# Loading tokens in runs of 4 or 5, and token-major attention tiles with DMA transposes from batch 3 on

## The chip, the cores and the metric

One core of one Trainium2 chip. The time is the device time of one launch in microseconds (us), here always in the fast state; a kernel's time is the median of its runs. Where two kernels are compared, the ratio is the mean time of one kernel's fast runs over the mean of the other's fast runs of the same rounds on the same chip, with a 95% interval. It is therefore not quite the ratio of the medians that are quoted beside it.

## The reference, cut to what matters

```
# q, k, v: 8 batches x 8 heads x 576 tokens x 64
kv  = einsum('bhsd,bhse->bhde', k, v)
out = einsum('bhsd,bhde->bhse', q, kv)
out = out / sqrt(mean(out*out, axis=-1) + 1e-6) * g_norm     # per token and head
x   = out as 4608 tokens x 512
h   = x @ w_in                                               # 512 -> 2048
g   = max(h, 0) + alpha * min(h, 0)
y   = g @ w_out                                              # 2048 -> 512
```

576 tokens are four and a half times 128, and the kernels work through the 4608 tokens in nine windows of 512. Batches and windows therefore do not line up: a window takes its tokens from one or two batches.

## The kernel before

All matrix products are in fp16. A head pair j is 128 of the 512 features. Attention for the next window is cut into small steps, which are strewn between the MLP units of the window at hand. A step is a transpose of q on TensorE (`t`), the product of k and v (`kv`), the output product (`ot`), or the sum of squares with the normalisation (`ssq`):

```
    def step_ot(w, j, pool=None):          # features on partitions
        ...
            nc.tensor.matmul(
                out=ot_ps[:, n0 - w * W : n1 - w * W], lhsT=kvs[b, j][:],
                rhs=qts[b, j][:, n0 - b * S : n1 - b * S], start=True, stop=True,
            )
        ...
        nc.scalar.activation(out=sq[:], in_=ot_ps[:], func=AF.Square)

    def ssq_mm(w, j):                      # sum of squares over partitions: a matmul with a mask
        nc.tensor.matmul(out=ssq_ps[:], lhsT=mask16[:], rhs=sq[:], start=True, stop=True)
        ... # Ln, Exp on ScalarE
```

One unit of the MLP is four matmuls for 128 features of h, a Relu on ScalarE (`m_sb`), the PReLU on VectorE (`gt`), and four matmuls of y for the window before. The window loop pops the steps behind the units:

```
            want = n * (g - first_g + 1) // (NF - 2 - first_g)
            while steps and n - len(steps) < want:
                steps.pop(0)()
```

The start brings in batch 0 in halves of four heads and works on each half as it comes (`regroup` copies a loaded half into the order that the matmuls need; `keep_warm(n)` issues n idle matmuls, whose result nobody reads):

```
    regroup(0, "q", 0, H // 2)
    step_t(0, 0, H_POOL)
    regroup(0, "k", 0, H // 2)
    step_t(0, 1, H_POOL)
    keep_warm(3)
    step_kv(0, 0)
    step_kv(0, 1, H_POOL)
    step_ot(0, 0)
    step_ot(0, 1)
    regroup(0, "q", H // 2, H)
    ... # transposes of the second half
    ssq_mm(0, 0)
    ssq_mm(0, 1)
    norm(0, 0)
    step_kv(0, 2)
    step_kv(0, 3, H_POOL)
    norm(0, 1)
```

## Time and profile before

| | before |
|---|---|
| time | 320.44 us, median of 3 runs (319.75 to 321.03) |
| profiled run | 319.12 us, span 317.4 us, mean granted TensorE clock 0.993 |
| start of window 2 | 79.35 us |
| start of window 2 to the last run of y matmuls | 218.57 us |

The last two rows cut the run in two: a start, in which engines wait for data and for each other, and a steady stretch, in which TensorE is full. The start in a few lines of the timeline of PE (start us, busy us, engine, line, operation, output<-inputs, shape; in brackets the idle time before it and who ended it):

```profile
9.75 1.25 PE L234 MATMUL qt_ps<-ident,qsb 128*128 128x128 f16 x10 [0.60 <-DVE qsb L146]
...
12.33 0.51 PE L249 MATMUL kv_ps<-vst,ksb 128*128 128x128 f16 x4
...
18.10 0.38 PE L323 MATMUL h_ps<-xt,w_in_sb 128*128 128x512 f16 x1
```

The first q work starts at 9.75 us, the first kv product at 12.33, the MLP at 18.10. The groups of PE instructions that the change cuts (line, engine, operation, shape, count | busy us, mean ns | idle us before, by releaser):

```profile
L234 PE MATMUL qt_ps<-ident,qsb 128*128 128x128 f16 x160 | 14.4, 225 | 1.9 <-DVE qsb L146 1.2 <-DVE kv_sb L257 0.8
L287 PE MATMUL ssq_ps<-sq_sb,mask 128*128 128x512 f16 x36 | 13.6, 378 | 6.7 <-ACT sq_sb L277 5.6 <-ACT rstd L289 1.1
```

The mean ns of one matmul (225, 378) is the length of its record, and records of neighbours overlap; what one costs in a row of them is read from starts, 56 and 216 ns.

### The profile page before, as it was taken

Reading aid. Unit: us, or ns where it says so; the run is one execution under the profiler, and the core shown is the slowest. Engines: PE = TensorE matmul, PEld = TensorE weight load, DVE = VectorE, ACT = ScalarE, POOL = GpSimd, SP = SyncE. Lnnn points to the kernel's source line nnn. Section 1 sums busy time; section 2 is a strip of 40 time slices with the busy share of each in tenths; the row PEclk is TensorE's granted clock in tenths of the full one; section 3 lists DMA queues with packets and bytes.
Section 4 is the critical chain, followed back from the end, with each engine's and each line's share of the span. In section 5 each row is a group of like instructions: output and inputs, shape, how many; then the busy total and the mean of one; then the engine's idle time right before and its main releaser. Section 6 shows DMA issues by size and latency. Waiting matters only on the chain.

```text
span 317.4 us, 4195 instructions
## 1 busy us (share of the span) xinstructions
PE 293.4 (92%) x1588; PEld 142.0 (45%) x1588; DVE 157.2 (50%) x267; ACT 173.4 (55%) x292; POOL 66.6 (21%) x74
## 2 busy tenths in 40 slices
PE   5668998898999999999999999999999999999994
PEld 1323453454455455545554455444544444444441
DVE  4547833666655554545464546454554445443300
ACT  2366546468466636674567456655665667444211
POOL 8434312737340541055005200000000000000000
PEclk9799999999999999999999999999999999999999
DMA  7999999998973859077715811000011111001132
GB/s 110 179 206 195 200 197 143 174 149 89 169 101 51 115 92 118 34 104 113 108 35 86 120 35 33 33 36 33 33 35 33 33 33 36 33 34 37 52 80 66
DMA packets 47621, 28.27 MB, mean 89 GB/s; under 512 B 14304, under 2 KB 42992, under 8 KB 47600
## 3 DMA queue, kind: packets, MB, share of 16 engines
q0 software_dynamic: 40320, 18.16, 45.7%
q1 hardware_dynamic: 7280, 9.84, 11.2%
q8 instruction: 12, 0.20, 0.3%
q14 instruction: 9, 0.07, 0.1%
HBM read 36.71 MB, written 9.44 MB: 145 GB/s over the span
## 4 chain that ended last, share of the span: by engine, by line
PE 85%; ACT 6%; DVE 4%; DMA 2%; issue 1%; SPq 1%; ACTq 0%
PE h_ps L323 37%; PE y_ps L345 36%; PE qt_ps L234 3%; PE kv_ps L249 3%; PE ssq_ps L287 3%; PE ot_ps L271 2%; DMA alpha_row<-in_moe_alpha_dram 2%; ACT rstd L289 2%; ACT sq_sb L277 1%; ACT rstd L292 1%; DVE gt L332 1%; DVE xt L298 1%; ACT m_sb L330 1%; SPq L100 1%; PE yb L345 1%
## 5 line engine op out<-in xcount | busy, mean ns | idle before, releaser
L332 DVE SCALAR_TENSOR_TENSOR gt<-m_sb,beta_sb,h_ps 128x512 f16<-128x512 f32 x144 | 106.8, 745 | 87.2 <-ACT m_sb L330 86.4
L323 PE MATMUL h_ps<-xt,w_in_sb 128*128 128x512 f16 x576 | 146.2, 379 | 2.9 <-DVE xt L298 1.7
L345 PE MATMUL y_ps<-w_out_sb,gt 128*128 128x512 f16 x528 | 134.8, 379 | 0.1
L330 ACT ACTIVATE m_sb<-h_ps 128x512 f32<-128x512 f32 x144 | 85.3, 594 | 80.4 <-PE h_ps L323 80.3
L345 PEld LDWEIGHTS <-gt 128*128 128x128 f16 x576 | 56.1, 98 | 67.1 <-issue 1.7
L323 PEld LDWEIGHTS <-w_in_sb 128*128 128x128 f16 x576 | 54.2, 98 | 64.2 <-issue 10.4
L298 DVE SCALAR_TENSOR_TENSOR xt<-ot_ps,g2col,rstd 128x512 f16<-128x512 f32 x36 | 27.0, 751 | 43.3 <-ACT rstd L292 43.2
L289 ACT ACTIVATE rstd<-ssq_ps,eps_t 128x512 f32<-128x512 f32 x36 | 24.7, 687 | 18.0 <-PE ssq_ps L287 17.9
L277 ACT ACTIVATE sq_sb<-ot_ps 128x512 f16<-128x512 f32 x36 | 21.3, 596 | 16.2 <-PE ot_ps L271 15.6
L352 ACT COPY y_sb<-y_ps 128x512 f32<-128x512 f32 x33 | 19.3, 586 | 18.4 <-PE y_ps L345 18.4
L292 ACT ACTIVATE rstd<-rstd 128x512 f32<-128x512 f32 x36 | 22.7, 629 | 1.1
L287 PE MATMUL ssq_ps<-sq_sb,mask 128*128 128x512 f16 x36 | 13.6, 378 | 6.7 <-ACT sq_sb L277 5.6
L129 POOL DMA_DIRECT2D vst<-in_v_dram x9 | 7.7, 860 | 50.4 <-PE kv_ps L249 48.6
L146 POOL COPY qsb<-qst 128x2048 f16<-128x2048 f16 x6 | 11.4, 1897 | 32.5 <-DMA qst<-in_q_dram 32.5
L249 PEld LDWEIGHTS <-ksb 128*128 128x128 f16 x160 | 11.6, 99 | 11.2 <-issue 4.2
L234 PE MATMUL qt_ps<-ident,qsb 128*128 128x128 f16 x160 | 14.4, 225 | 1.9 <-DVE qsb L146 1.2
L234 PEld LDWEIGHTS <-qsb 128*128 128x128 f16 x160 | 11.6, 101 | 9.4 <-DVE qsb L146 2.4
L243 DVE COPY qt_sb<-qt_ps 128x576 f16<-128x576 f16 x32 | 14.4, 451 | 2.5 <-PE qt_ps L234 2.5
L271 PE MATMUL ot_ps<-qt_sb,kv_sb 128*128 128x512 f16 (+7 forms) x64 | 13.5, 286 | 0.8 <-DVE kv_sb L257 0.7
L249 PE MATMUL kv_ps<-vst,ksb 128*128 128x128 f16 x128 | 12.3, 220 | 1.8 <-DVE qt_sb L243 1.8
L146 POOL COPY ksb<-kst 128x2048 f16<-128x2048 f16 x6 | 11.4, 1903 | 11.9 <-DMA kst<-in_k_dram 11.9
L257 DVE TENSOR_TENSOR kv_sb<-kv_ps,mask 128x128 f16<-128x128 f32 x32 | 9.0, 285 | 3.8 <-PE kv_ps L249 3.8
(43 smaller groups left out, 92.6 us busy)
## 6 DMA issues: line engine op xcount, KB each, us to landing
out_dram<-y_sb SPq DMA_DIRECT2D x40, 128.0 KB, 2.4
out_dram<-y_sb SPq DMA_DIRECT2D x16, 256.0 KB, 2.3
kst<-in_k_dram POOLq DMA_DIRECT2D x7, 512.0 KB, 6.9
qst<-in_q_dram POOLq DMA_DIRECT2D x7, 512.0 KB, 10.1
vst<-in_v_dram POOLq DMA_DIRECT2D x7, 512.0 KB, 8.4
w_in_sb<-in_moe_w_in_dram POOLq DMA_DIRECT2D x4, 512.0 KB, 14.7
w_out_sb<-in_moe_w_out_dram POOLq DMA_DIRECT2D x4, 512.0 KB, 16.1
qst<-in_q_dram POOLq DMA_DIRECT2D x2, 256.0 KB, 7.5
```

Source lines behind the costliest of these rows:

```text
L146: (eng or nc.vector).tensor_copy(out=dst, in_=src)
L234: nc.tensor.matmul(out=qt_ps[:, t * P : (t + 1) * P], lhsT=qs(t), rhs=ident16[:], is_transpose=True, start=(t == 0), stop=(t == NT - 1),)
L249: nc.tensor.matmul(out=kv_ps[:], lhsT=ks(t), rhs=vs(t), start=(t == 0), stop=(t == NT - 1),)
L277: nc.scalar.activation(out=sq[:], in_=ot_ps[:], func=AF.Square)
L287: nc.tensor.matmul(out=ssq_ps[:], lhsT=mask16[:], rhs=sq[:], start=True, stop=True)
L289: nc.scalar.activation(out=rstd[:], in_=ssq_ps[:], func=AF.Ln, bias=eps_t[:], scale=inv_d,)
L292: nc.scalar.activation(out=rstd[:], in_=rstd[:], func=AF.Exp, bias=0.0, scale=-0.5)
L298: nc.vector.scalar_tensor_tensor(out=xts[w, j][:], in0=ot_ps[:], scalar=g2col[:], in1=rstd[:], op0=ALU.mult, op1=ALU.mult,)
L323: nc.tensor.matmul(out=h_ps[:], lhsT=w_in_blk(c, g), rhs=xts[w, c][:], start=(c == 0), stop=(c == NC - 1),)
L330: nc.scalar.activation(out=m_sb[:], in_=h_ps[:], func=AF.Relu, scale=-1.0)
L332: nc.vector.scalar_tensor_tensor(out=gt[:], in0=m_sb[:], scalar=beta_sb[:, g : g + 1], in1=h_ps[:], op0=ALU.mult, op1=ALU.add,)
L345: nc.tensor.matmul(out=y[:], lhsT=gts[w, g][:, a * P : (a + 1) * P], rhs=w_out_blk(g), start=(g == 0), stop=(g == NF - 1),)
```

## The change

Its intent: the loads become two per tensor, in which each partition takes a run of 5 tokens (the first 320 tokens) or 4 (the other 256), in place of runs of 4 and single tokens. From batch 3 on, q is transposed by a DMA instead of TensorE, the output product is made with tokens on partitions (a tile is 128 tokens x 512 features), the sum of squares becomes a reduction on VectorE, GpSimd spreads the factor `rg`, VectorE multiplies, and a second DMA transposes the tile into the layout that the MLP needs (`xm`). The loads of a batch, their regrouping and the transpose of q are placed in different units. Load buffers go from three sets to two. The start is rewritten: q of batch 0 comes uncast over SyncE's queue, and is cast on VectorE.

```
+    def load(b, nm, h0=0, h1=H, dst=None, eng=None):
+        ...
+            out=st[0:REM].rearrange("p h t d -> p h (t d)"),
+            in_=src[:, 0:LONG, :].rearrange("h (p t) d -> p h (t d)", t=NT),
+        ...
+            out=st[REM:P, :, 0:TPP, :].rearrange("p h t d -> p h (t d)"),
+            in_=src[:, LONG:S, :].rearrange("h (p t) d -> p h (t d)", t=TPP),
...
+    def transpose_q(b):
+        nc.sync.dma_start_transpose(out=qtms[b][:], in_=bufs[b % NBUF]["q"][:]...)
+
+    def tile_a(b, t):                       # four 128-column matmuls, tokens on partitions
+        ot_ps = ps_o.tile([P, H, D], FP32, name="otm_ps", tag=f"o{n_tile[0] % 3}")
+        ... # Square on ScalarE
+    def tile_b(b, t): ...                   # tensor_reduce on VectorE
+    def tile_c(b, t): ...                   # Ln, Exp on ScalarE, rg on GpSimd
+    def tile_d(b, t):
+        nc.vector.tensor_mul(out=x[0:n], in0=ot_ps[0:n], in1=rg[0:n])
+        ... # nc.sync.dma_start_transpose into xm
...
+        for i in range(len(todo) + 3):      # unit i of the window
+            m = []
+            for k, fn in ((3, tile_d), (0, tile_a), (1, tile_b), (2, tile_c)):
+                if 0 <= i - k < len(todo):
+                    m.append(lambda fn=fn, x=todo[i - k]: fn(*x))
+            d = i >= 3
+            steps.append((m[:d], m[d:]))    # (between h and y, behind y)
+        if w < B:
+            for j in range(NPAIR):
+                steps[j // 2][j % 2].append(lambda j=j: step_kv(w, j))
...
+    regroup(0, "q", 0, HH, src=q32[0])      # the start
+    step_t(0, 0, H_POOL)
+    step_t(0, 1, H_POOL)
+    regroup(0, "q", HH, H, src=q32[1])
+    step_t(0, 2, H_POOL)
+    step_t(0, 3, H_POOL)
+    regroup(0, "k", 0, HH)
+    keep_warm(3)
+    step_kv(0, 0)
+    ...
+    step_kv(0, 2)
+    step_kv(0, 3, H_POOL)
+    norm(0, 0)
+    norm(0, 1)
```

All four `kv_ps` of a window use the one PSUM buffer `(ps_s, "s")`; the tiles turn over three, `o0` to `o2`.

## The prediction

> **What bounds the kernel now.** The page's first two parts say which engine and when; the columns of the first are busy us, share of the span, instructions.
>
> ```profile
> PE 293.4 (92%) x1588; PEld 142.0 (45%) x1588; DVE 157.2 (50%) x267; ACT 173.4 (55%) x292; POOL 66.6 (21%) x74
> ...
> PE   5668998898999999999999999999999999999994
> ...
> PEclk9799999999999999999999999999999999999999
> ```
>
> PE is full from about slice 11 (80 us) on and has gaps only in the first ten slices of 7.9 us; the clock is granted everywhere but in one early slice. No other engine is near full. The chain that ended last agrees: 85% of it is PE.
>
> ```profile
> PE 85%; ACT 6%; DVE 4%; DMA 2%; issue 1%; SPq 1%; ACTq 0%
> PE h_ps L323 37%; PE y_ps L345 36%; PE qt_ps L234 3%; PE kv_ps L249 3%; PE ssq_ps L287 3%; PE ot_ps L271 2%; DMA alpha_row<-in_moe_alpha_dram 2%; ACT rstd L289 2%; ACT sq_sb L277 1%; ACT rstd L292 1%; DVE gt L332 1%; DVE xt L298 1%; ACT m_sb L330 1%; SPq L100 1%; PE yb L345 1%
> ```
>
> 73% is the MLP itself (h and y), which the change leaves alone. qt, ssq and ot, 8% together, are what it touches. The waits of PE from 79.6 us (start of window 2; a window is 512 tokens, 16 units of 4 h and 4 y matmuls) to 298 us have one entry (total us, times, longest):
>
> ```profile
> PE ssq_ps L287 <- ACT sq_sb L277: 3.4, 5, 0.7
> ```
>
> So for 218 us every PE instruction taken away shortens the run, and every new PE wait lengthens it. I read the prices from one unit of the timeline (start us, us):
>
> ```profile
> 148.49 1.03 PE L323 MATMUL h_ps<-xt,w_in_sb 128*128 128x512 f16 x4
> ...
> 149.35 1.03 PE L345 MATMUL y_ps<-w_out_sb,gt 128*128 128x512 f16 x4
> 149.55 0.60 ACT L330 ACTIVATE m_sb<-h_ps 128x512 f32<-128x512 f32 x1 [1.41 <-PE h_ps L323]
> ...
> 150.18 0.75 DVE L332 SCALAR_TENSOR_TENSOR gt<-m_sb,beta_sb,h_ps 128x512 f16<-128x512 f32 x1 [1.05 <-ACT m_sb L330]
> 150.22 0.44 PE L234 MATMUL qt_ps<-ident,qsb 128*128 128x128 f16 x5
> ...
> 150.50 1.03 PE L323 MATMUL h_ps<-xt,w_in_sb 128*128 128x512 f16 x4
> ```
>
> Starts, not durations, give the cost: four 512-column matmuls take 149.35 - 148.49 = 0.863 us, five 128-column ones 150.50 - 150.22 = 0.28 us (56 ns each). The second use of these lines: gt ends 2.44 us after its h began, while PE has finished h and y at 1.73 us. DVE thus finishes a unit 0.7 us after PE is through with it. That costs nothing now, but anything PE must get from DVE behind that gt comes late.
>
> At the end of each window there is one real stall, in two lines:
>
> ```profile
> 139.75 0.38 PE L271 MATMUL ot_ps<-qt_sb,kv_sb 128*128 128x256 f16 x2
> 140.81 0.38 PE L287 MATMUL ssq_ps<-sq_sb,mask 128*128 128x512 f16 x1 [0.69 <-ACT sq_sb L277]
> ```
>
> ssq could issue at 139.97 and issues at 140.81: 0.84 us, in five windows (2 to 6), 4.2 us.
>
> **What the Trainium skill says.** "TensorE: Matmul & The Clock Gate", Back-to-back issue gap, gives N/2.4 + 2.5 ns for an isolated matmul (216 ns at 512 columns, 56 at 128) and a longer 81 ns at 128 columns within a stream with weight loads. The trace has 216 and 56 within such a stream, so I use those. "PSUM — Partial Sum Buffer", Engine vs sequencer instructions, says ScalarE, VectorE and GpSimdE queues are strict FIFO; the trace agrees (the qt copy of this unit starts only as gt ends), and the rival below rests on it. "Advanced Engine Details and Errata", X-Bar Transpose (TRN2), calls transposing DMAs as fast as regular ones and expects 350-400 GB/s; "VectorE: DVE Perf Modes", The three transpose paths, has 1309 ns for one 128x128 block by DMA against 390 by TensorE. No DMA transpose is in this trace.
>
> **The change part by part.**
>
> (a) PE work removed. Batches 3 to 7 no longer transpose q on PE: 5 x 20 x 56 ns = 5.6 us. Windows 3 to 8 no longer sum squares with a matmul (DVE reduces instead): 24 x 216 ns = 5.2 us, less two 384-column ones for the tail of batch 2 (0.33): 4.85. The out product changes form: before, 24 x 512 columns (5.2 us); after, 25 tiles x 4 x 56 ns plus four 192-column ones = 5.9 us: +0.7. Sum -9.7 us, all on the path.
>
> (b) The stall at the window's end goes with ssq: -4.2 us.
>
> (c) New waits, from the order in which the changed kernel issues. In windows 2 to 6 the four kv products now sit two in a unit (one between h and y, one after y) but share one PSUM buffer, freed by a DVE multiply queued behind that unit's gt. In the first unit: gt ends at 2.44 us, the multiply (285 ns) at 2.73, kv can go at 2.80; PE is ready at 0.863 + 0.28 + 0.863 + 0.23 (the tile) = 2.24. Stall 0.56 us, twice per window, five windows: +5.6.
>
> (d) The same with the token tiles. They rotate over three buffers; tile i needs the product of tile i-3 (DVE, TensorTensor 128x512 out of PSUM; estimate 0.70 us from 285 ns for 128 columns and 745 for gt), issued in the same unit behind gt. There ACT also carries the square (0.60) and two small activations (estimate 0.2 each) of the unit before, so m_sb starts at about 1.22 instead of 1.06, gt ends at 2.6, the product at 3.3, PE goes on at 3.37. It was ready at 1.73: stall 1.65 us. Windows 2 to 7 prepare 3, 4, 5, 4, 5, 4 tiles; each beyond a window's third stalls: 7 x 1.65 = +11.5.
>
> (e) In window 2 the POOL queue issues a batch's six loads (about 0.86 us each, 5 us) before the second tile's POOL product; DVE waits behind it, and with three h buffers in hand I put what reaches PE at +0.9. The fp16 regroup on DVE grows from 2048 to 2560 columns (685 ns to about 0.85) twice in window 0: +0.3.
>
> (f) The start. q of batch 0 comes uncast over the SP queue, without the 256-byte remainder rows that now go first. DMA writes 206 GB/s in its third slice, from fp32 sources of twice that; half of q and half of k, 1.18 MB, should then land near 5.5 us, where the first regroup began at 9.27. The fp32 regroup is slower (estimate 1.5 us for 1280 columns against 0.42 to 0.80) and there are two in line, so I keep 1.5 us of the gain: -1.5.
>
> (g) Off the path: ACT does 12 activations of 0.6 to 0.7 us per window before, about 4 of 0.6 and 9 short ones after; DVE work stays about equal; a batch takes 3072 descriptors instead of 4608 (runs of 5 and 4 tokens instead of 4 and 1). The loads were hidden from window 2 on: 0.
>
> Sum: -9.7 - 4.2 + 5.6 + 11.5 + 0.9 + 0.3 - 1.5 = +2.9. From 320.4 that is 323.3. That the code was evidently laid out on purpose, perhaps with waits I overrate, makes me shade it to **322.5 us**.
>
> **The rivals.**
> 1. The removed PE work pays in full: PE follows its own count and the new waits are absorbed. For it: PE is the only full engine. Against it: the DVE lag of 0.7 us in the unit above, with single or triple PSUM buffers handed back in the same unit. Time: 320.4 - 13.9 - 1.5 = 305.
> 2. The DMA transposes become the bound. Per window 0.65 MB of q and 0.59 MB of tiles go through SP's queue with the stores. At the speed of plain transfers that is some 4 us plus fixed costs in 30; q is requested in unit 13 and needed 5 to 7 units (9 to 12 us) later. If instead each 128x128 block cost 1.3 us in series, 38 blocks would take 50 us per window, PE would wait about 15 to 20 us in each of five windows: 400 us or more. I give anything of this sort 10%.
> 3. POOL or ACT sets the tile chain: POOL's product of 128x512 must be done within about 1.3 us (its fp16 copy of 2048 columns takes 1.9 us). If it takes 2, the stalls of (d) grow by about 0.7 us each: 327.
>
> **Range and chances.** (c) and (d), 17 us, are the largest and least tested terms; halving them gives 314, and the start is uncertain by 2 us either way. A late POOL or q transpose gives 327 to 332. I take 314 to 331. Faster than 314: 0.19, mostly rival 1 in part; slower than 326.8: 0.25, rivals 2 and 3; within 2%: 0.56.
>
> **What the changed profile would show.** Right: PE's 128-column transposes drop from 160 to 60, ssq matmuls from 36 to 14; PE waits on DVE: kv on the masked multiply about ten times at 0.3 to 0.6 us, and the tile matmul on the row product seven times at 1.2 to 1.7 us; no waits of ssq on sq in windows 3 on. The windows from 3 to 6 last 32.4 and 34.3 us in turn, against 32.4 before. Wrong: if those DVE waits are missing, (c) and (d) fail and the time nears 305; if PE waits for DMA on a tile or on the first h of a window, rival 2 holds; if the first h matmul starts later than 18.1 us, (f) fails.

## The result, and the profile after

| | before | after |
|---|---|---|
| time, median | 320.44 us | 325.14 us (4 runs, 323.8 to 325.56) |
| ratio | | 1.014, interval 1.0104 to 1.0176: within 2% |
| profiled run: time, span, clock | 319.12, 317.4, 0.993 | 325.0, 323.2, 0.989 |
| start of window 2 | 79.35 us | 83.12 us |
| start of window 2 to the last run of y | 218.57 us | 220.34 us |
| from there to the end | 19.48 us | 19.74 us |

The span grew by 5.80 us: 3.77 at the start, 1.77 in the steady stretch, 0.26 at the end. The profiled run of before was 1.3 us better than its median, so the medians are only 4.7 apart and the start's share of them is nearer 2.7 than 3.8.

The page of the changed kernel, busy time of the engines and the row of PE:

```profile
PE 287.1 (89%) x1526; PEld 136.2 (42%) x1526; DVE 165.3 (51%) x274; ACT 155.8 (48%) x298; POOL 94.2 (29%) x101
...
PE   4476997987999998999699979997899899999993
```

62 matmuls are gone and PE is busy for 6.3 us less; its row now has dents of 6 and 7 in the middle, where it read 9 throughout before. The chain that ended last is no longer mostly PE:

```profile
issue 38%; DMA 31%; PE 19%; POOL 8%; DVE 2%; ACT 0%; POOLq 0%; DVEq 0%; ACTq 0%
```

This must not be read as "DMA bounds it". The waits of PE from window 2 to the last y (us in total, times, longest) are the check, and a DMA is named in them for 0.5 us only:

```profile
PE otm_ps L343 <- DVE xrow L376: 9.3, 7, 1.4
PE kv_ps L234 <- DVE kv_sb L242: 2.4, 8, 0.4
PE h_ps L435 <- DVE gt L444: 0.4, 1, 0.4
PE kv_ps L234 <- DMA vst<-in_v_dram: 0.3, 1, 0.3
PE h_ps L435 <- DMA xm<-xrow: 0.2, 1, 0.2
```

The stalls of ssq are gone, and five kinds of new waits stand in their place. The largest, seven times, is the token tile waiting for the row product. One of them in the timeline of all engines:

```profile
122.86 1.03 PE L435 MATMUL h_ps<-xm,w_in_sb 128*128 128x512 f16 x4
...
124.05 0.58 ACT L442 ACTIVATE m_sb<-h_ps 128x512 f32<-128x512 f32 x1
...
124.66 0.75 DVE L444 SCALAR_TENSOR_TENSOR gt<-m_sb,beta_sb,h_ps 128x512 f16<-128x512 f32 x1 [0.72 <-ACT m_sb L442]
...
125.33 0.68 DVE L376 TENSOR_TENSOR xrow<-otm_ps,rg 128x512 f16<-128x512 f32 x1
...
126.07 0.40 PE L343 MATMUL otm_ps<-kv_sb,qtm 128*128 128x128 f16 x4 [1.32 <-DVE xrow L376]
```

PE was through with h and y at 122.86 + 1.73 = 124.59 us, and could go on at 126.07: 1.48 us. By starts like these the seven waits are 1.42 to 1.56 us, 10.5 in all (the view counts 9.3, since it starts each wait only where the record of the last matmul ends). By the same measure the kv products wait 3.8 us for the masked multiply in nine places, a kv product 0.8 us for v in two, an h 0.6 us for gt and another 0.3 for a tile's transpose: 16.0 us of new waits. The steady stretch became 1.8 us longer, so the work and the stall taken away were worth 16.0 - 1.8 = 14.2 us. (This is a difference; the run best, below, confirms it.)

What went from PE (the groups of its transposes and of its sums of squares, 160 and 36 before):

```profile
L219 PE MATMUL qt_ps<-ident,qsb 128*128 128x128 f16 x60 | 5.1, 222 | 5.8 <-DVE qsb L107 5.0 <-DVE kv_sb L242 0.8
...
L276 PE MATMUL ssq_ps<-sq_sb,mask 128*128 128x512 f16 x12 | 4.5, 378 | 3.5 <-ACT sq_sb L266 2.4 <-ACT rstd L278 1.1
```

The third number of each is its idle time over the whole run: the 5.0 us that qt waits for `qsb` are at the start, and 4.0 of them are one wait. Here is the start on PE; beside it, from the timeline of DVE, the cast that it waits for:

```profile
7.67 0.73 PE L219 MATMUL qt_ps<-ident,qsb 128*128 128x128 f16 x10 [0.67 <-DVE qsb L107]
12.40 0.85 PE L219 MATMUL qt_ps<-ident,qsb 128*128 128x128 f16 x10 [4.00 <-DVE qsb L107]
...
20.09 1.01 PE L260 MATMUL ot_ps<-qt_sb,kv_sb 128*128 128x512 f16 x2 [1.04 <-DVE xt L287]
20.89 2.56 PE L435 MATMUL h_ps<-xt,w_in_sb 128*128 128x512 f16 x6
```

```profile
11.51 0.83 DVE L107 CAST qsb<-q 128x1280 f16<-128x1280 f32 x1 [2.53 <-DMA q<-in_q_dram]
```

The first q work starts 2.1 us sooner than before, but the second half of q is there only at 11.51 us, everything else stands behind it in PE's order, and the MLP begins 2.8 us later. Its first six matmuls take 2.4 us by starts, some 0.40 us each, against 0.216 at full speed. The clock in stretches of 2 us (stretch, length, busy us and instructions of PE, its weight loads, DVE, ACT and POOL, then granted clock, DMA share, GB/s):

```profile
10.00:12.00 2.00, 0.00 (x0) 0.00 (x0) 0.49 (x1) 0.00 (x0) 0.74 (x1) 1.00 0.84 100
12.00:14.00 2.00, 1.60 (x13) 0.95 (x13) 1.45 (x4) 0.00 (x0) 0.74 (x1) 0.72 0.91 120
14.00:16.00 2.00, 1.94 (x13) 1.16 (x11) 0.59 (x3) 0.00 (x0) 0.00 (x0) 0.50 1.30 189
...
18.00:20.00 2.00, 0.95 (x11) 0.67 (x11) 1.20 (x4) 1.89 (x4) 1.14 (x2) 0.92 1.24 206
20.00:22.00 2.00, 1.91 (x5) 0.65 (x5) 0.73 (x2) 1.08 (x2) 0.76 (x1) 0.50 1.24 206
```

After the idle 4 us the clock is granted at half. The Trainium skill, "TensorE: Matmul & The Clock Gate", Part 1, has the array fall to half rate after an idle window of about 3.4 us and come back after a busy one of that length. This trace agrees for the first fall (idle from 8.40 to 12.40, then 0.72 and 0.50). But that dip is over by 17 us, and the six h matmuls stand in a second one, from about 19.7 to 23.1 us, though no idle time of PE behind the first was longer than 1.04 us: what made the clock fall there is not shown. The kernel before has one dip (0.50 from 10 to 12 us), and it is over at 14.

Two durations settle the other rivals, the times from issue to landing of the DMA transposes and the product on GpSimd:

```profile
xm<-xrow SPq DMA_TRANSPOSE x28, 3.0
qtm<-qsb SPq DMA_TRANSPOSE x5, 4.2
```

```profile
L367 POOL TENSOR_TENSOR rg<-ss,g_all 128x512 f32<-128x512 f32 (+1 forms) x25 | 25.9, 1049 | 111.8 <-ACT ss L365 107.5 <-DVE gt L444 4.2
```

A whole q, 20 blocks of 128 x 128, lands 4.2 us after its issue, and `rg` is done in 1.05 us.

### The profile page after: what moved, and what is told of

Read it like the earlier page. It is cut to its first block, busy times and chain, and to the rows that moved or that the text cites. A ratio compares the mean times of both kernels' runs of the same rounds, so it can differ in the third digit from the quotient of the medians.

```text
span 323.2 us, 4236 instructions
## 1 busy us (share of the span) xinstructions
PE 287.1 (89%) x1526; PEld 136.2 (42%) x1526; DVE 165.3 (51%) x274; ACT 155.8 (48%) x298; POOL 94.2 (29%) x101
## 4 chain that ended last, share of the span: by engine, by line
issue 38%; DMA 31%; PE 19%; POOL 8%; DVE 2%; ACT 0%; POOLq 0%; DVEq 0%; ACTq 0%
DMA qst<-in_q_dram 20%; PE y_ps L457 12%; PE h_ps L435 7%; POOL rg L367 5%; DMA vst<-in_v_dram 5%; DMA w_in_sb<-in_moe_w_in_dram 4%; DMA kst<-in_k_dram 2%; POOL kst L97 1%; POOL kst L101 1%; POOL qst L97 1%; DVE xrow L376 1%; DVE gt L444 1%; DVE ss L355 0%; ACT y_sb L464 0%; PE otm_ps L343 0%
## 5 line engine op out<-in xcount | busy, mean ns | idle before, releaser
L435 PE MATMUL h_ps<-xm,w_in_sb 128*128 128x512 f16 x384 | 98.6, 379 | 0.2 <-DMA xm<-xrow 0.2
L367 POOL TENSOR_TENSOR rg<-ss,g_all 128x512 f32<-128x512 f32 (+1 forms) x25 | 25.9, 1049 | 111.8 <-ACT ss L365 107.5
L435 PE MATMUL h_ps<-xt,w_in_sb 128*128 128x512 f16 x192 | 48.6, 386 | 3.2 <-DVE gt L444 1.7
L349 ACT ACTIVATE sqm_sb<-otm_ps 128x512 f32<-128x512 f32 (+1 forms) x25 | 14.9, 596 | 21.2 <-PE otm_ps L343 21.2
L376 DVE TENSOR_TENSOR xrow<-otm_ps,rg 128x512 f16<-128x512 f32 (+1 forms) x25 | 17.0, 681 | 6.0 <-POOL rg L367 6.0
L107 POOL COPY ksb<-kst 128x2560 f16<-128x2560 f16 x6 | 13.9, 2317 | 18.4 <-DMA kst<-in_k_dram 18.4
L107 POOL COPY qsb<-qst 128x2560 f16<-128x2560 f16 x6 | 13.9, 2321 | 13.7 <-DMA qst<-in_q_dram 13.7
L355 DVE TENSOR_REDUCE ss<-sqm_sb 128x8 f32<-128x512 f32 (+1 forms) x25 | 16.9, 674 | 0.0
L287 DVE SCALAR_TENSOR_TENSOR xt<-ot_ps,g2col,rstd 128x512 f16<-128x512 f32 x12 | 8.9, 750 | 15.0 <-ACT rstd L281 15.0
L266 ACT ACTIVATE sq_sb<-ot_ps 128x512 f16<-128x512 f32 x12 | 6.9, 592 | 19.3 <-PE ot_ps L260 19.3
L278 ACT ACTIVATE rstd<-ssq_ps,eps_t 128x512 f32<-128x512 f32 x12 | 8.2, 684 | 7.4 <-PE ssq_ps L276 7.3
```

What stands on the lines that cost most here:

```text
L107: (eng or nc.vector).tensor_copy(out=bufs[b % NBUF][nm][:, :, h0:h1, :].rearrange("p t h d -> p h t d"), in_=stages[b % NBUF][nm][:, h0:h1 ...
L349: nc.scalar.activation(out=sq[0:n], in_=ot_ps[0:n], func=AF.Square)
L355: nc.vector.tensor_reduce(out=ss[0:n], in_=sq[0:n], op=ALU.add, axis=mybir.AxisListType.X,)
L367: nc.gpsimd.tensor_tensor(out=rg[0:n], in0=ss[0:n].unsqueeze(2).to_broadcast([n, H, D]), in1=g_all[0:n].unsqueeze(1).to_broadcast([n, H, D ...
L376: nc.vector.tensor_mul(out=x[0:n], in0=ot_ps[0:n], in1=rg[0:n])
L435: nc.tensor.matmul(out=h_ps[:], lhsT=w_in_blk(c, g), rhs=xt_of(w, c), start=(c == 0), stop=(c == NC - 1),)
```

## The experiments

The theory after the result: the steady stretch gained 14.2 us and lost 16.0 to buffers handed back behind `gt`; the start lost some 3 us of its own. Rivals: the waits are only where the time shows, and it would show elsewhere without them; for the start, PE's order, the clock, or the transfers. Edits are against the changed kernel unless said. All runs were correct; before measured 319.4 to 320.0 us beside them.

### kv_buf: a second PSUM buffer for the kv products

```
-                steps[j // 2][j % 2].append(lambda j=j: step_kv(w, j))
+                pool = (ps_o, kv_tag) if w > NB_PE and j % 2 else (ps_s, "s")
+                steps[j // 2][j % 2].append(lambda j=j, pool=pool: step_kv(w, j, pool))
```

`kv_tag` is the tile buffer that is free in these units, `f"o{(n_tile[0] + 2) % 3}"` at the start of the window.

> The changed kernel, but from window 3 on the second and fourth kv product of a window write to a second PSUM buffer. Theory (the kv products wait for one shared buffer behind gt on DVE): in windows 3 to 6 the waits of kv on the masked multiply, 2.9 us by start times, are gone, and the time falls from 325.1 to 322.2 us. Rival (DVE is simply late in these units, so the wait only moves to the next PE instruction that needs DVE): the tile matmul's waits grow by as much, time within 1 us of 325.1.

Measured: 322.11 us (6 runs), ratio to before 1.0062 (1.0031 to 1.0094); the steady stretch 216.94 us against 220.34. The waits of PE:

```profile
PE kv_ps L234 <- DVE kv_sb L242: 0.6, 2, 0.4
```

The two left are those of window 2, which the edit leaves out. The tile waits stay at 9.3. The kv waits were real time: 3.4 us by the steady stretch, 2.5 by the ratios (1.014 - 1.0062, of 320).

### tile_gap: the fourth and fifth tile of a window one unit later

```
-        for i in range(len(todo) + 3):
+        at = {n + (n >= 3): x for n, x in enumerate(todo)}
+        for i in range(max(at) + 4):
+            ... # tile_d of the tile at unit i - 3, and tile_a, tile_b, tile_c as before
...
-            if g == LOAD_G and w + 2 < B:
+            if g == LOAD_G - (w > 2) and w + 2 < B:
```

The product that frees the buffer is then asked for one unit ahead of the tile that needs it. Loads move one unit forward so as not to meet the later tiles.

> The changed kernel with one empty unit between the third and the fourth token tile of a window (loads one unit earlier in windows 3 to 5). Theory (the fourth and fifth tile wait for a PSUM buffer whose product sits behind gt in the same unit): all seven waits of the tile matmul on the row product, 10.5 us by start times, vanish; 314.7 us. Rival (DVE cannot keep up with gt, product and reduction in one unit at all): the waits come back elsewhere, on h or kv, and less than half of 10.5 us is gained: above 320.

Measured: 315.29 us (4 runs), ratio 0.9858 (0.9815 to 0.99). No tile waits are left in the view; the steady stretch is 209.96 us, 10.4 less. One unit of slack took the whole of term (d) away; the kv waits on DVE rose from 2.4 to 3.0, while the wait for v is gone.

### before_ssq: the stall of the kernel before, taken away alone

The edit is to the kernel before. In windows 2 to 6 there are 16 steps for 14 units, so two units take two steps each; the second of them now comes one unit earlier, so that the last ssq of a window is one unit behind its square.

```
             want = n * (g - first_g + 1) // (NF - 2 - first_g)
+            if 1 < w < B - 1:
+                want = min(g + 1 + (g >= 6) + (g >= 12), n)
```

> The kernel before, with its last two attention steps of windows 2 to 6 in different units (the second doubled unit one earlier). Tests the size of the stall at a window's end that the change removed: theory 0.84 us by start times in each of five windows, 4.2 us: 316.2 us. Rival (the stall only moves into the next instruction that waits): 320.

Measured: 316.3 us, ratio 0.9911 (0.9868 to 0.9955); steady stretch 215.03 us against 218.57, and no waits of PE left in the view. The stall is worth 3.5 us there, of 4.2 predicted. It was to be had without the change.

### loads_only: the loads, buffers and start of the change, the window steps of the kernel before

The edit keeps the new loads and the new start, sets the first batch of tiles beyond the last one, and puts the old loop over steps behind the units. There are no DMA transposes in it.

```
-    NB_PE = 3
+    NB_PE = NW
...
+            want = n * (g + 1) // (NF - 2)
+            while steps and n - len(steps) < want:
+                steps.pop(0)()
```

> Only the first part of the change: runs of 5 and 4 tokens, two sets of buffers and the new start, but all batches prepared on PE as before, no DMA transposes. Theory (the loads cost only at the start, +3.8 us; the token tiles save 14.2 us of PE time and end-of-window stalls and add 16 us of waits): 324.3 us, windows of 32.4 us as before. Rival (the larger runs or the two buffers make waits of their own in the windows): above 327; rival (the token tiles are what costs at the start): 320.5.

Measured: 322.8 us, ratio 1.0101 (1.0056 to 1.0147). The steady stretch is 218.57 us, to the hundredth that of before, and window 2 starts at 84.48. So the new loads cost nothing once the MLP runs, and the start alone costs 3.2 us (1.0101 of 320), with an interval of 1.8 to 4.7. The start is a loss that has nothing to do with tiles or transposes.

### start_order: kv and output products of the first heads ahead of q's second half

```
     step_t(0, 1, H_POOL)
-    regroup(0, "q", HH, H, src=q32[1])
-    step_t(0, 2, H_POOL)
-    step_t(0, 3, H_POOL)
     regroup(0, "k", 0, HH)
...
     step_ot(0, 1)
+    regroup(0, "q", HH, H, src=q32[1])
+    step_t(0, 2, H_POOL)
+    step_t(0, 3, H_POOL)
```

> The changed kernel with the order of the kernel before in its first microseconds: kv and the out product of the first four heads ahead of the transposes of the second half of q. Loads as in the change. Theory (PE and DVE stand in line behind the second half of q, which landed at 11.5 us): first h matmul at about 18.5 us instead of 20.9, time about 322.6. Rival (everything waits for the total of the first loads whatever the order): first h stays at 20.5 or later, time 325.

Measured: 326.13 us, ratio 1.0178 (1.0141 to 1.0215): a miss, as the rival had it. PE idles as it did, now for v:

```profile
12.27 1.23 PE L234 MATMUL kv_ps<-vst,ksb 128*128 128x128 f16 x10 [2.93 <-DMA vst<-in_v_dram]
```

v's first half is there at about 12.2 us, as in the kernel before (12.33), and the clock, which fell in the idle time, stayed at 0.50 from 12 to 24 us. The first h is at 20.89, as with the order of the change. The order by itself gains nothing here; the low clock takes its part in that, and start_fix, below, takes it out.

### start_queue: the same, and q's second half on the queue of k and v

```
-    load(0, "q", HH, H, q32[1], nc.sync)
+    load(0, "q", HH, H, q32[1])
```

> As start_order, and the second half of q is loaded over the POOL queue, behind the first halves of k and v, instead of over SP's queue from the first moment. Theory (two queues share the DMA engines, so the half that is needed last delayed the ones needed first): first halves land 1 to 2 us sooner, first h matmul at 16 to 17 us, time about 320.5. Rival (the sum of the first loads decides): same as start_order.

Measured: 326.82 us, ratio 1.0232 (1.0204 to 1.026): a miss again, and slower than the change (the two intervals, 1.0204 to 1.026 and 1.0104 to 1.0176, do not meet). First h at 21.43 us; first kv at 12.09, where start_order had 12.27 and 1 to 2 us were expected.

### all_three: kv_buf, tile_gap and start_queue together

> The changed kernel with kv_buf, tile_gap and start_queue together. Theory (three separate waits on one path, each worth what it is worth alone): 325.1 - 2.9 - 10.5 - 4.6 = 307.1 us, faster than both kernels. Rival (the waits hide one another): above 312.

Measured: 313.12 us, ratio 0.9797 (0.9765 to 0.9829): faster than both kernels, though short of what was expected, since its third part lost time instead of saving any. The steady stretch is 206.79 us: 13.55 less than in the change, close to 3.4 + 10.4, so the two repairs add up.

### start_warm: idle matmuls over the wait at the start

```
     regroup(0, "q", HH, H, src=q32[1])
+    keep_warm(16)
     step_t(0, 2, H_POOL)
```

> The changed kernel with 16 extra dummy matmuls where PE sat idle for 4 us (8.4 to 12.4 us). Theory of a secondary cost (the clock granted to PE fell after that idle time, so the six h matmuls at 20.9 us took 0.43 us each instead of 0.22, and others before them too): with PE kept busy these run at 0.22 and about 1.3 us are gained, 323.8. Rival (the start waits for loads, clock or not): first h matmul at the same 20.9 us and the time within 0.5 us of 325.1.

Measured: 323.81 us (6 runs), ratio 1.0127 (1.0094 to 1.016). In its profiled run the clock is 1.00 throughout and window 2 starts at 80.78, 2.3 us sooner than in the change. The timed gain is small, 0.4% with overlapping intervals. Each run records its granted clock, and these show why:

| clock of the run | before | after | start_warm |
|---|---|---|---|
| 0.984 to 0.989 | 319.8 to 321.6 (13 runs) | 325.0 to 325.6 (3 runs) | none |
| 0.993 to 0.996 | 318.9 to 319.6 (6 runs) | 323.8 (1 run) | 322.8 to 325.1 (4 runs) |

(The column of before has the runs beside start_warm and beside start_fix. Two runs of start_warm at 0.998 and 0.999, 323.97 and 322.68 us, and three of before at 0.98 and 1.00 fall in neither row.) At a like clock the change is still some 4.5 to 5 us behind. A step of 0.01 in the clock goes with 1 to 1.5 us in both kernels, and the clocks of the two profiled runs are 0.993 and 0.989. So the clock takes time at the start of either kernel, but in the timed runs it is a small part of what sets them apart. How large a part stays open: in the profiled runs, window 2 of start_warm starts 1.4 us later than in the kernel before, in place of the 3.8 of the change.

### start_fix and warm_norm: order, clock and norms

start_fix is start_order with 16 instead of 3 idle matmuls ahead of the first kv product, and both norms ahead of the last kv products; warm_norm is start_warm with the same move of the norms.

```
-    keep_warm(3)
+    keep_warm(16)
     step_kv(0, 0)
...
+    norm(0, 0)
+    norm(0, 1)
     step_kv(0, 2)
     step_kv(0, 3, H_POOL)
-    norm(0, 0)
-    norm(0, 1)
```

> Edit against the changed kernel: three things at the start. The kv and out products of the first two head pairs go ahead of the transposes of q's second half; 16 instead of 3 idle matmuls run just ahead of the first kv product, to hold the clock while v is still on its way; the two norms go ahead of the third and fourth kv product, as they did before the change. Theory A (the lost 3.8 us at the start are idle time of PE behind q's second half, plus the half clock that follows it, plus an out product that waits 1.04 us for a norm): first kv still at about 12.2 us because v can't land sooner, clock 1.00 from there on, first h at about 18.3 us, start of window 2 at 79.5 to 80.5 us instead of 83.1, time 321.5. Theory B (the transfers of the first batch and the weights set the start, whatever PE does): first h still at 19.5 or later, time 323.5 to 325.

> Edit against the changed kernel: the 16 idle matmuls ahead of the third transpose (as in the run start_warm), and the two norms ahead of the third and fourth kv product; the order of the products stays that of the change. It tells the order of the norms from the clock. If the norm order is worth what its wait shows, first h at about 18.6 us (19.57 in start_warm less 1.0) and a time of 322.8; if that wait is hidden by another one, first h stays at about 19.5 us and the time at about 323.8.

Measured: start_fix 324.09 us, ratio 1.0132 (1.0108 to 1.0155); warm_norm 325.55, ratio 1.0186 (1.0151 to 1.0221). start_fix misses its theory A, and theory B (transfers) holds: first h at 19.5 or later, 323.5 to 325 us. warm_norm misses both of its forecasts; in its profiled run q's first half itself came late (first q work at 9.34 us against 7.67), which is not explained. In start_fix the clock is 1.00 in every stretch and the first h still comes at 20.11, and the move of the norms was a mistake:

```profile
19.66 0.60 PE L260 MATMUL ot_ps<-qt_sb,kv_sb 128*128 128x512 f16 x2 [1.65 <-DVE kv_sb L242]
```

The second norm waits for ScalarE until 18.66 us, and the masked multiply, which the output product needs, stands behind it in DVE's queue. A wait of 1.04 us was traded for one of 1.65.

### start_as_before: start_fix with the norms in the order of the kernel before

```
     norm(0, 0)
-    norm(0, 1)
     step_kv(0, 2)
     step_kv(0, 3, H_POOL)
+    norm(0, 1)
```

> Edit against the changed kernel: the run start_fix with one difference, the norms in the order of the kernel before: the first norm ahead of the third and fourth kv product, the second behind them. In start_fix both norms stood in front of the masked multiplies on DVE, the second norm waited for its rstd until 18.66 us, and the out product waited 1.65 us for the multiply behind it. If the order of the small DVE work is what is left of the loss at the start, the multiplies start at about 18.2 us, first h comes at about 18.9 us instead of 20.11, window 2 starts at about 80 us, and the time is about 322.7 (1.4 less than start_fix). If it is the landing of v (12.95 against 12.33 us in the kernel before) and nothing else, the time stays at 324.

Measured: 324.83 us (6 runs), ratio 1.016 (1.0133 to 1.0188): a miss, nearer to the second forecast. But now the first kv is at 12.21, the first output product at 13.04 and the third at 18.01 us, against 12.33, 13.29 and 17.66 in the kernel before, and PE meets something new (waits of PE from 16 to 24 us):

```profile
PE h_ps L435 <- DMA w_in_sb<-in_moe_w_in_dram: 0.9, 1, 0.9
...
PE kv_ps L234 <- DMA vst<-in_v_dram: 0.8, 1, 0.8
```

(The line left out, 0.8 us of ssq for ScalarE, is in the kernel before as well.) Both are transfers: v's second half, and the first block of the MLP's weights, which is there only at about 19.6 us. In the kernel before the MLP ran on that block from 18.10 us and did not wait for it. So once PE's order is that of the kernel before, the transfers are late, and up to the first h (19.61 against 18.10 us) they are what is left. Behind it comes a second loss, which the waits do not show: the clock.

```profile
18.00:20.00 2.00, 1.07 (x3) 0.33 (x4) 0.89 (x2) 1.09 (x2) 0.19 (x2) 0.65 1.24 207
20.00:22.00 2.00, 2.00 (x6) 0.73 (x5) 0.00 (x0) 0.00 (x0) 0.60 (x1) 0.50 1.24 206
```

It stays at 0.50 until about 29 us, though no idle time of PE from 8 to 19.6 us was longer than 0.93 us, and the first twelve h matmuls run at half speed. Window 2 starts at 82.77, 3.4 us later than before: 1.5 of it are there at the first h, and the rest goes with this stretch (from the first h to window 2 it is 63.2 us, against 61.1 to 61.3 in the kernel before, start_warm and start_fix, whose clock is full there). In the timed runs with a clock of 0.992 to 0.995 the times are 323.5 to 325.0, so the dip is not the whole loss.

The timeline of POOL, which issues these loads, shows it on its side (a load's issue is an instruction there). First the kernel before, then the changed one:

```profile
5.98 2.39 POOL L166 DMA_DIRECT2D w_in_sb<-in_moe_w_in_dram  x3
9.30 0.74 POOL L166 DMA_DIRECT2D w_in_sb<-in_moe_w_in_dram  x1 [0.94 <-DMA kst<-in_k_dram]
```

```profile
6.83 1.09 POOL L169 DMA_DIRECT2D w_in_sb<-in_moe_w_in_dram  x1
9.10 0.74 POOL L169 DMA_DIRECT2D w_in_sb<-in_moe_w_in_dram  x1 [1.18 <-DMA kst<-in_k_dram]
...
12.40 0.74 POOL L169 DMA_DIRECT2D w_in_sb<-in_moe_w_in_dram  x1 [0.94 <-DMA vst<-in_v_dram]
```

Before, the four weight loads are out by 10 us; in the change, with eight loads ahead of them on that queue instead of six, three of them wait for an older one to land, and the last goes out at 12.4. In that time, from 10 to 14 us, the transfers of the change move 100 and 120 GB/s, those of the kernel before 166 and 196. That the two go together is an inference: no run here changes the number of loads or their order against the weights alone.

### best: kv_buf, tile_gap and start_as_before together

> Edit against the changed kernel: all that paid, together. The second PSUM buffer for the kv products (kv_buf, -2.9), the fourth and fifth tile one unit later (tile_gap, -10.4 with no tile wait left), and the start of start_as_before (-2.4). Sum from 324.9: 309. If the kv gain and the tile gap overlap (both take waits from the same unit), 310 to 311. The run all_three, with a start that lost 1.5 us, gave 313.1; less than 2 us below it would mean that the start is not what it lacked.

Measured: 308.62 us (6 runs, 307.58 to 311.06), ratio 0.9632 (0.9611 to 0.9653): 3.7% faster than the kernel before. A stretch of a window's first unit, in which the change had its kv waits (timeline of PE, profiled run):

```profile
116.07 0.44 PE L234 MATMUL kv_ps<-vst,ksb 128*128 128x128 f16 x5
116.35 1.03 PE L460 MATMUL y_ps<-w_out_sb,gt 128*128 128x512 f16 x4
117.21 0.39 PE L343 MATMUL otm_ps<-kv_sb,qtm 128*128 128x128 f16 x4
117.43 0.44 PE L234 MATMUL kv_ps<-vst,ksb 128*128 128x128 f16 x5
```

Not one line has a bracket, nor has any up to 130 us: PE goes from step to step. The steady stretch is 205.82 us, 14.5 less than in the change. The time is where it was expected, but part of that is luck: the sum counted 2.4 us for a start that gained nothing by itself, and the medians of best and start_as_before are 16.2 apart where the steady stretches (205.82 and 220.97) account for 15.2. The clock goes with the rest: at 0.991 to 0.995 the means are 309.1 (3 runs) and 324.4 (4 runs), 15.3 apart, and best itself spans 3.5 us, from a clock of 1.00 down to 0.983.

best also confirms the 14.2 us. Its stretch is 12.75 us shorter than that of the kernel before, and by starts 1.5 us of waits are left in it, all in window 2: with no waits it would be 14.2.

A fair measure of the tiles is not the kernel before but before_ssq, which takes the stall away with two lines of code: by the two ratios best is 2.8% faster than that (0.9632 / 0.9911; the two were not run side by side).

## Why the prediction was right or wrong

The total was near, 322.5 against 325.14 us, but in part by luck: two errors of opposite sign partly cancelled. (The shading from the sum, 323.3, to 322.5 led away from the result.) The steady part was predicted at +4.1 us ((a) to (d), and 0.9 of (e)) and measured +1.8; the start was predicted at -1.2 ((f), and 0.3 of (e)) and measured +3.8 in the profiled pair, +3.2 in loads_only.

- **(a) and (b), work and stall removed.** Predicted 13.9 us, measured 14.2 as the new waits less the net loss. The stall alone measured 3.5 in before_ssq, against 4.2. The prediction took one window's stall, 0.84 us, for all five; by the same starts they fall from 0.91 to 0.69, 4.0 in all.
- **(c) the kv products behind gt.** The mechanism was right, and kv_buf took it away. The size was 5.6 (ten stalls of 0.56) and measured 3.8 in nine places: most were 0.46, and a tenth fell on a wait for v instead.
- **(d) the fourth and fifth tile.** Right in its mechanism, its count of seven, and nearly in size: 1.42 to 1.56 us each instead of 1.65, 10.5 in all instead of 11.5. The estimates it was built on were a little high: the product ended 3.15 us after the unit's first h, not 3.3. tile_gap removed 10.4. The predicted check, windows of 32.4 and 34.3 us in turn, shows as 32.1 and 33.8.
- **(e)** The wait that reached PE in window 2 was 0.57 instead of 0.9, on the path foreseen: GpSimd begins `rg` only at 103.45 us, behind the loads, and the row product on DVE waits 3.4 us for it. The larger regroup took 0.82 us, twice, instead of 0.685: 0.3 us on DVE as said; whether they reach PE is not shown.
- **(f) the start: here the prediction failed.** The step was that half of q and half of k "should then land near 5.5 us", from which it took a gain of 1.5. The first cast began at 6.78, not at 5.5, and still 2.5 us sooner than the first regroup before; its 0.83 us was less than the 1.5 allowed. (The sum let uncast q come at twice the 206 GB/s that DMA wrote. An estimate with what is written, 0.59 MB of q as fp32 and 0.29 MB of k as fp16, takes 4.3 us at that rate in place of 2.9, which would account for the difference; no run tests it.) The gain was thus there, and it was lost at once. The step priced the first member of a chain and took that for the price of the chain: q's second half came at 11.5 us, v's first half at 11.2 to 13.1 in the runs that waited for it, and the weights later than before. The predicted check said so: the first h is at 20.89, later than 18.1. Which landing holds PE up depends on its order: q's second half in the change, v in start_order, v's second half and the weights in start_as_before. No order tried brings the first h below 19.57 us (start_warm), and how much of the loss is landings and how much the clock stays open.
- **Rival 1** fell: the new waits were real. It was nearly right about what was to be had: best is 308.6, the rival said 305. **Rival 2** fell with 4.2 us for a q and 0.5 us of DMA waits. **Rival 3** fell with `rg` at 1.05 us, within its 1.3.

Two statements of the Trainium skill bear on the start. "TensorE: Matmul & The Clock Gate", Part 1, led to the runs with idle matmuls: its rule of a fall after an idle window of about 3.4 us fits the first dip of the change (4.00 us idle), and does not cover the falls in start_as_before and best, near 19 and 20 us, where no idle time of PE in the 6 us before was longer than 1 us. The time hardly followed the clock. "DMA: Bandwidth & Descriptors", SWDGE vs HWDGE vs iDMA, says that only GpSimd's queue can cast in flight; this is why q, once moved to SyncE's queue, arrives as fp32 and needs the cast of 0.83 us on VectorE. The trace agrees: those loads land in an fp32 tile, k and v over GpSimd's queue in fp16.

**Open:** why v's first half never lands before some 12 us in the orders tried, apart from start_queue inside all_three (first kv at 11.18); which part of the new loads delays the weights; and what makes the clock fall near 19 us. The steady part is settled by runs, the start is not.

## What to carry to other kernels

When work leaves the engine that is full, ask who gives back each buffer that the remaining work writes into, and where that instruction stands in its engine's queue: here a release behind the unit's `gt` cost a wait in every unit that had no spare buffer. A spare buffer for the kv products and one unit of distance for the tiles turned the change from a loss of 1.4% into a gain of 3.7% (in best, whose new start gained nothing by itself). A start is a chain of landings: to have its first member sooner, or the engine's order better, moved the time little here.

## What the Trainium skill lacked or had wrong

- "TensorE: Matmul & The Clock Gate", Back-to-back issue gap: for streams with weight loads it gives 81 ns at 128 columns and 131 ns at 512. In both kernels such streams run at 56 and 216 ns by their starts (the tile at 122.64 us and the h behind it at 122.86: four matmuls in 0.22 us; an h and the y behind it 0.86 us apart), as its formula for isolated matmuls says. The measurement decides.
- "VectorE: DVE Perf Modes", The three transpose paths: 1309 ns for one 128x128 block by DMA. It does not say how several blocks of one transpose go together; the 350-400 GB/s of "Advanced Engine Details and Errata", X-Bar Transpose (TRN2), does. Here 20 blocks (0.66 MB) landed 4.2 us after the issue, 0.21 us a block or 156 GB/s with the fixed part in it; the transposes of one tile, of up to four blocks, took 3.0 us (medians).
- "PSUM — Partial Sum Buffer", Engine vs sequencer instructions: the strict FIFO is right, but no page puts a price on a PSUM buffer that is given back behind other work. Here it was 0.46 us for most of the kv products and 1.42 to 1.56 us for a tile.
- "TensorE: Matmul & The Clock Gate", Part 1: it names short idle times between groups of matmuls as something that makes the clock swing, but no page says how busy PE must be. With PE busy for 1.0 to 2.0 of every 2 us the clock stayed at 0.50 for 12 us in start_order; in start_as_before it fell near 19 us after 5 us in which PE was busy for 1.07 to 1.21 of every 2.
